# Turning a recurrent state on TensorE: eight transposes per unit in place of sixteen products with the identity, with a new written-out order

## The chip, the cores and the metric

The kernel runs on one core of one Trainium2 chip. The time is the device time of one execution in microseconds, as the median over runs. TensorE (PE in the profile) multiplies; its weight loads have a row of their own (PEld). VectorE is DVE, ScalarE is ACT, GpSimd is POOL, and SyncE (SP) issues the transfers. TensorE writes to PSUM only; ACT and DVE read PSUM and copy to SBUF.

## The reference

Two blocks follow one another. The first is a linear recurrence with a 40x40 state for each of 4 batches and 8 heads, over 768 steps:

```python
for t in range(S):
    kt, vt, rt = (k[:, :, t], v[:, :, t], r[:, :, t])
    wt, at, bt = (w[:, :, t], a[:, :, t], b[:, :, t])
    y[:, :, t] = np.einsum('bhd,bhde->bhe', rt, state)
    Sa = np.einsum('bhde,bhe->bhd', state, at)
    state_decay = state * wt[:, :, None, :] - np.einsum('bhd,bhe->bhde', Sa, bt)
    state = state_decay + np.einsum('bhd,bhe->bhde', vt, kt)
```

The second is an MLP on the 3072 tokens of 320 channels that come out: `h = x @ w_in` (320 to 2048), `g = h * sigmoid(1.702 h)`, `g @ w_out` (2048 to 320). All is fp32.

## The kernel before

The recurrence is done in 24 units: 12 blocks of 64 time steps by 2 pairs of batches. A unit `i` holds 16 heads (2 batches of 8), so the state of a unit is 16 matrices of 40x40. Each unit goes through the same steps. `decay` forms the running products of w (tiles FT, GT, G, wch, wz). `prep` scales a, k, b and forms the scores A and RV. `inverse` inverts a triangular 64x64 matrix per head in five levels (ps_N, ps_level, then ps_Q and ps_T for the off-diagonal part). `solve` brings in the state of the unit two before (the same batches, the block before): it turns the state (ps_zT), reads it with r (ps_rz), forms the known side (ps_B), solves (ps_X), and makes from it both the output and the next state (ps_y). The output x goes to DRAM and comes back with channels on the partitions (x_dram, xT_all). After every second unit the MLP of the block, `mlp`, can run: 40 pieces of ps_up, a gelu on ACT per ten of them, and 16 pieces of ps_down. The weights arrive in 8 pieces at the start and are put into fp32 by ACT, DVE and POOL (lines 489 to 507).

All products on TensorE are cut to 64 rows by at most 64 columns, so that four run at once, one in each quarter of the array. A product in fp32 shows as two loads and two matmul records. Every product but the transposes of the new version goes through the helper `mm`, line 343 (301 after), so the profile tells them apart by their tiles.

The steps around the change are in `solve`, lines 890 to 917. The raw state of the unit two before (zraw, in slots of 40 columns) is scaled by wz and written into zr, whose rows of 104 hold 64 columns for the read-out and 40 for the state. `state_turned` multiplies 16 blocks of zr, 64 rows by 40 columns, with a 64x40 identity into ps_zT, 40 rows on each half of the partitions. Two copies (line 904) bring it to zT, and `read_state` multiplies zT with r. zr itself is also an operand of ps_B.

Nothing is scheduled at run time. Each step is a task of the class `Plan` (`plan.add`), with the engines that may do it, what it reads and writes, and the PSUM pair that it holds; there are four such pairs, and a task that needs one waits in its engine's queue until it is free. The program issues the tasks in one list, and each engine runs its part of the list in that order; semaphores hold an instruction until what it needs is there. In the version before, `Plan.order` (line 103) makes the list: it steps through a model of the engines, and at each step takes the able task of lowest rank. `paced` (line 223) spreads the MLP's tasks, and `moved` (line 242) shifts ranks, releases and engines of groups of tasks by a table, `FOUND` (line 260). DMAs are issued by SP alone, in the list's order: `load_w`, `load`, the weights, x out and back, and the stores of the result.

Of the kernel before, what the change touches and what calls it, by code (L numbers as in the profile page):

```python
# [22 lines left out]
ACT = mybir.ActivationFunctionType  # L23
# [26 lines left out]
class Task:  # L50
    def __init__(self, rank, engines, fn, pair, most, size):
        self.instr, self.sbuf, self.table = engines.pop("instr", -Plan.EVENTS) + Plan.EVENTS, engines.pop("sbuf", False), engines.pop("table", None)
        self.rank, self.fn, self.pair, self.most, self.size = rank, fn, pair, most, size
        self.engines = self.may = engines
        self.after, self.then, self.release = set(), [], 0.0
        self.load = False


class Plan:

    BLOCK, FETCH, AHEAD = 256, 3460.0, 300.0
    FIRST, EVENTS = 63, 0.24
    BESIDE, LARGE, BESIDE_LARGE = 0.35, 327700, 0.5
    COLD, WINDOW, SHARE = 2.0, 2600.0, 0.45
    SWITCH = 1290.0
    DELAY = {"PE": 300.0, "DVE": 60.0, "ACT": 60.0, "POOL": 150.0, "SP": 800.0}  # L70

    BEGIN = {"PE": 0.0, "ACT": 3300.0, "DVE": 6500.0, "POOL": 10000.0, "SP": 800.0}
    LATENCY, RATE, SPREAD = 2010.0, 417.0, 1.3
# [29 lines left out]
    def order(self):  # L103
        for n, t in enumerate(self.tasks):
            t.n, t.left, t.ready, t.then = n, len(t.after), 0.0, []
        for t in self.tasks:
            for o in t.after:
                o.then.append(t)
        free = dict(self.BEGIN)
        pairs = [0.0] * self.pairs  # L110
        held, users = {}, {k: len(v) for k, v in self.of_pair.items()}
        coming = [(t.release, t.n) for t in self.tasks if not t.left]
        heapq.heapify(coming)
        able, now, wire, out, many = [], 0.0, 0.0, [], set()
        running, last, worked = [], {}, []
        table = "exp"

        def fits(t, margin=0.0):
            if t.pair is None or t.pair in held:
                return True  # L120
            clear = sum(p <= now - margin for p in pairs)
            if t.most is None:

                return clear > len({o.pair[0] for o in able if o.most is not None and o.pair not in held and not any(k[0] == o.pair[0] for k in many)})
            return clear > 0 and sum(k[0] == t.pair[0] for k in many) < t.most

        issued, begun, shared = self.FIRST, 0.0, 0.0

        def fetch(at):
            took = self.FETCH  # L130
            for _ in range(3):
                took = self.FETCH + sum(w * max(0.0, min(y, at + took) - max(x, at)) for x, y, w in running[-10:])
            return took

        def unread(t, e):

            return max((x + 60.0 for o, x in last.get(t.pair, {}).items() if o != e), default=0.0) if t.pair is not None and e != "PE" else 0.0

        def takes(t, start):

            busy = sum(max(0.0, y - max(x, start - self.WINDOW)) for x, y in worked[-60:])
            return t.engines["PE"] * (self.COLD if busy < self.SHARE * self.WINDOW else 1.0)

        def fetched(t, start):

            ns = takes(t, start) / t.instr
            at, left, block = start, t.instr, begun
            room = self.BLOCK - issued % self.BLOCK
            while left >= room:
                at += room * ns  # L150
                left -= room
                at = block = max(at, block + fetch(block))
                room = self.BLOCK
            return at + left * ns, block

        def ahead(t):

            return (issued % self.BLOCK + t.instr) * fetch(begun) / self.BLOCK - (now + takes(t, now) - begun)

        while coming or able:  # L160
            while coming and coming[0][0] <= now:
                able.append(self.tasks[heapq.heappop(coming)[1]])
            able.sort(key=lambda t: (t.rank, t.n))
            took = None
            for e in free:
                if free[e] <= now:
                    took = None
                    took = next((t for t in able if e in t.may and fits(t) and unread(t, e) <= now), None)
                    if took and e == "PE" and ahead(took) > self.AHEAD:

                        took = next((t for t in able if e in t.may and fits(t) and ahead(t) < min(self.AHEAD, ahead(took))), took)
                    if took:
                        break
            if not took:
                later = [x for x in (*free.values(), *pairs, *(unread(t, e) for t in able for e in t.may)) if now < x < float("inf")]
                later += [coming[0][0]] if coming else []
                if not later:
                    return out
                now = min(later)
                continue  # L180
            t = took
            able.remove(t)
            t.engine = e
            end = now + t.engines[e]
            if e == "ACT" and t.table:
                t.load, table = t.table != table, t.table
                end += self.SWITCH if t.load else 0.0
            if e == "PE":
                end, begun = fetched(t, now)
                worked.append((now, min(end, now + takes(t, now))))  # L190
                issued += t.instr
            if e == "POOL" or e == "DVE" and t.sbuf:

                shared = max(now, shared) + t.engines[e]
                end = max(end, shared)
            free[e] = end
            if e == "SP":
                wire = max(wire, end + self.LATENCY)
                running.append((wire, wire + self.SPREAD * t.size / self.RATE, self.BESIDE_LARGE if t.size > self.LARGE else self.BESIDE))
                end = wire = running[-1][1]  # L200
            if t.pair is not None:
                if e != "PE":
                    last.setdefault(t.pair, {})[e] = end
                if t.pair not in held:
                    held[t.pair] = next(i for i, p in enumerate(pairs) if p <= now)
                    pairs[held[t.pair]] = float("inf")
                    if t.most is not None:
                        many.add(t.pair)
                t.bank = held[t.pair]
                users[t.pair] -= 1  # L210
                if not users[t.pair]:
                    many.discard(t.pair)
                    pairs[t.bank] = end + self.DELAY[e]
            for o in t.then:
                o.ready = max(o.ready, end + (0.0 if o.engines.keys() == {e} else self.DELAY[e]))
                o.left -= 1
                if not o.left:
                    heapq.heappush(coming, (max(o.ready, o.release), o.n))
            t.start = now
            out.append(t)  # L220
        return out

    def paced(self, groups, rounds, window, share):


        best = None
        for n in range(rounds):
            out = self.order()
            end = max(t.start + t.engines[t.engine] for t in out)
            if best is None or end < best[0]:  # L230
                best = end, [(t, {**vars(t)}) for t in out]
            for g, then in zip(groups, groups[1:]):
                whole, done, begin = sum(t.engines["PE"] for t in g), 0.0, g[0].ready
                for t in g:
                    new = begin + share * (then[0].ready - begin) * done / whole - window
                    t.release = new if n == 0 else 0.5 * (t.release + new)
                    done += t.engines["PE"]
        for t, kept in best[1]:
            vars(t).update(kept)
        return [t for t, _ in best[1]]  # L240

    def moved(self, moves):

        groups = {}
        for t in self.tasks:
            key = (t.fn.__code__.co_firstlineno, t.rank, tuple(sorted(t.engines)), t.pair)
            groups.setdefault(key, []).append(t)
# [12 lines left out]
FOUND = """  # L260
# [31 lines left out]
def rwkv7_gelu_quick(ctx: ExitStack, tc: tile.TileContext, time_d, v_d, w_d, wc_d, ak_d, b_d, rv_d, w_in, w_out, out):  # L292
# [144 lines left out]
    for t in zT_t:  # L437
        nc.gpsimd.memset(t[:, DM:], 0.0)
# [742 lines left out]
```

## Time and profile before

| | |
|---|---|
| median of 3 runs | 687.27 us (685.94, 687.27, 688.87) |
| span of the profiled execution | 685.1 us (its own time isn't given beside it) |
| mean granted TensorE clock | 0.989 |
| PE busy | 649.1 us, 95% |
| DVE, ACT, POOL busy | 459.0, 323.5, 184.5 us |
| ps_up, ps_down in the chain that ended last | 29%, 30% |
| ps_zT in it | 1% |
| first and last ps_up | 73.3 and 665.8 us |

How to read it: the span goes from the first to the last instruction. A row of a group gives the engine, the operation, the tiles out<-in, the shapes and the count, then the busy time and the mean of one; behind the bar stands the engine's idle time just before and what ended it. A matmul's shape begins with the tile of the array (64*64 is 64 rows by 64 columns). A wait row says which instruction waited for which, with the total, the number of times and the longest.

### The profile page before, as it was taken

What the parts mean: (1) busy time and instruction counts of PE and PEld (TensorE: products, weight loads), DVE (VectorE), ACT (ScalarE), POOL (GpSimd) and SP (SyncE); (2) the same over time, 40 slices, a digit from 0 to 9 for tenths busy, and PEclk for the clock granted to TensorE, in tenths of its full rate; (3) what the DMA queues carried; (4) which work ended last, traced back from release to release, by engine and by line L of the source; (5) the groups of instructions that cost most, each with busy time, mean ns of one, the idle gap of its engine ahead of it and who ended that gap; (6) DMA issues with size and microseconds to landing.
All of it is one profiled execution on the core that took longest, in us unless ns stands there. A gap on an engine that the chain in (4) does not pass through costs nothing.

```text
span 685.1 us, 42187 instructions
## 1 busy us (share of the span) xinstructions
PE 649.1 (95%) x19488; PEld 563.2 (82%) x19488; DVE 459.0 (67%) x916; ACT 323.5 (47%) x670; POOL 184.5 (27%) x215
## 2 busy tenths in 40 slices
PE   3657999999999999999999999999999999999997
PEld 3556888997899899988888897788788799899895
DVE  6686989767867767857785677867666766675001
ACT  4566633454555664564455445355354454262110
POOL 5354546324123212323213130322411421300000
PEclk9989999999999999999999999999999999999999
DMA  7993434414414413432404413413411411200100
GB/s 238 314 318 118 163 119 129 122 33 127 124 42 116 144 34 107 133 90 85 132 21 125 137 40 111 145 37 115 138 40 55 136 52 43 70 14 17 56 12 20
DMA packets 35312, 69.73 MB, mean 102 GB/s; under 512 B 5440, under 2 KB 14656, under 8 KB 35136
## 3 DMA queue, kind: packets, MB, share of 16 engines
q1 hardware_dynamic: 35136, 67.03, 32.6%
q8 instruction: 153, 2.51, 1.5%
q14 instruction: 23, 0.19, 0.1%
HBM read 59.15 MB, written 7.86 MB: 98 GB/s over the span
## 4 chain that ended last, share of the span: by engine, by line
PE 90%; DVE 3%; DMA 2%; issue 2%; ACT 1%; POOL 0%; SPq 0%; ACTq 0%; DVEq 0%
PE ps_down L343 30%; PE ps_up L343 29%; PE ps_level L343 9%; PE ps_y L343 5%; PE ps_B L343 5%; PE ps_X L343 3%; PE ps_A L343 2%; PE ps_N L343 2%; PE ps_RV L343 2%; PE ps_rz L343 1%; PE ps_zT L343 1%; PE ps_cum L343 1%; PE ps_T L343 1%; DMA rv<-in_rv 1%; DMA extra<-in_w_out 1%
## 5 line engine op out<-in xcount | busy, mean ns | idle before, releaser
L343 PE MATMUL ps_up<-xT_all,w_sb 64*64 64x256 f32 x3840 | 252.4, 377 | 1.0 <-issue 0.8
L343 PE MATMUL ps_down<-w_sb,g 64*64 64x320 f32 x3072 | 240.5, 430 | 0.5 <-issue 0.3
L343 PEld LDWEIGHTS ps_up<-xT_all,w_sb 64*64 64x64 f32 x3840 | 171.7, 133 | 15.9 <-issue 1.9
L343 PEld LDWEIGHTS ps_down<-w_sb,g 64*64 64x64 f32 x3072 | 136.1, 133 | 36.3 <-issue 1.1
L755 POOL TENSOR_TENSOR EX<-ES,quads 128x512 f32<-128x512 f32 x31 | 41.7, 1345 | 117.7 <-DVE ES L748 76.5
L1034 ACT ACTIVATE g<-ps_up 128x1024 f32<-128x1024 f32 x48 | 49.2, 1026 | 49.0 <-PE ps_up L343 48.6
L797 ACT COPY W<-ps_level 128x512 f32<-128x512 f32 x56 | 32.8, 586 | 69.3 <-PE ps_level L343 67.6
L343 PEld LDWEIGHTS ps_level<-W,EX 64*64 64x64 f32 x2560 | 59.4, 134 | 5.7 <-ACT EX L753 0.2
L799 DVE TENSOR_TENSOR E<-two,ps_level 128x256 f32<-128x256 f32 x80 | 33.1, 415 | 35.7 <-ACT W L797 32.0
L343 PE MATMUL ps_level<-W,EX 64*64 64x64 f32 (+1 forms) x2560 | 56.4, 217 | 0.0
L753 ACT ACTIVATE EX<-ES,quads 128x256 f32<-128x256 f32 x80 | 36.3, 501 | 32.5 <-DVE ES L748 31.9
L665 POOL TENSOR_TENSOR ak<-ak,FT 128x512 f32<-128x512 f32 x16 | 20.6, 1288 | 76.4 <-DMA ak<-in_ak 62.3
L343 PE MATMUL ps_level<-PT,EX 64*64 64x64 f32 (+2 forms) x1280 | 33.1, 236 | 8.3 <-DVE EX L769 4.5
L343 PEld LDWEIGHTS ps_level<-PT,EX 64*64 64x64 f32 x1280 | 30.9, 139 | 11.8 <-issue 6.5
L937 ACT COPY B<-ps_B 128x416 f32<-128x416 f32 (+1 forms) x35 | 17.2, 491 | 47.2 <-PE ps_B L343 47.0
L748 DVE STREAM_TRANSPOSE ES<-E 128x256 f32<-128x256 f32 x80 | 35.2, 442 | 4.4
L343 PE MATMUL ps_y<-M,bh 64*64 64x104 f32 (+1 forms) x768 | 35.1, 247 | 0.1
L343 PE MATMUL ps_y<-RV,kh 64*64 64x104 f32 (+1 forms) x768 | 35.1, 247 | 0.0
L999 POOL TENSOR_TENSOR x<-zr,FT 128x128 f32<-128x128 f32 x48 | 25.0, 552 | 29.7 <-DVE zr L989 14.2
L673 POOL TENSOR_TENSOR kh<-time,G 128x320 f32<-128x320 f32 x19 | 16.8, 887 | 52.4 <-PE ps_y L343 39.2
L343 PE MATMUL ps_B<-RV,A 64*64 64x104 f32 (+1 forms) x768 | 29.3, 252 | 1.4 <-issue 1.4
L343 PEld LDWEIGHTS ps_B<-RV,A 64*64 64x64 f32 x768 | 25.9, 137 | 5.4 <-issue 1.6
(136 smaller groups left out, 1111.0 us busy)
## 6 DMA issues: line engine op xcount, KB each, us to landing
time<-in_time SPq DMA_DIRECT2D x24, 320.0 KB
ak<-in_ak SPq DMA_DIRECT2D x48, 160.0 KB
rv<-in_rv SPq DMA_DIRECT2D x48, 160.0 KB
xT_all<-x_dram SPq DMA_DIRECT2D x48, 160.0 KB
wc<-in_wc SPq DMA_DIRECT2D x20, 264.0 KB
logw<-in_w SPq DMA_DIRECT2D x24, 160.0 KB
RV<-in_v SPq DMA_DIRECT2D x24, 160.0 KB
b<-in_b SPq DMA_DIRECT2D x48, 80.0 KB
```

Source lines behind the costliest of these rows:

```text
L343: nc.tensor.matmul(o, lhsT, rhs, start=start, stop=True, skip_group_check=True)
L665: plan.add(R, {"DVE": 690.0, "POOL": 1270.0, "sbuf": True}, lambda t: of(t.engine).tensor_mul(ahT(), ahT(), FT_of(i)), reads=T("ak", "FT") ...
L673: plan.add(R + 4, {"POOL": 870.0, "DVE": 490.0, "sbuf": True}, lambda t, n=n, dst=dst: of(t.engine).tensor_mul(dst(i)[:, :, :D], by_head(t ...
L748: plan.add(rank, dve(256), lambda t: nc.vector.transpose(ES(n), source(t)), writes=[key("ES", n, 6)], **reads)
L753: nc.scalar.activation(dst[:, :, h], ES(n), ACT.Copy, scale=quads[:, h, :1])
L755: of(t.engine).tensor_mul(dst, ES(n).unsqueeze(2).to_broadcast([128, 8, 2, 32]), quads.unsqueeze(1).to_broadcast([128, 8, 2, 32]))
L797: plan.add(rank, any2(512), lambda t: copy(t.engine)(tiles_of(W(n + 1)), blocks(psum(t, ""), 64)), writes=[key("W", n + 1, 5)], pair=pair)
L799: plan.add(rank, dve(256), lambda t: nc.vector.tensor_sub(tiles_of(E(n + 1)), every(two32, [128, 2, 4, 32]), blocks(psum(t, ""), 64)[:, :, ...
L937: plan.add(R, any2(4 * wide), lambda t: copy(t.engine)(dst(), some(psum(t, "")[:, :, :208])), writes=[("Bv", i)] if x and c > 0 else T("B" ...
L999: of(t.engine).tensor_mul(x[:, b ^ u, b], both(i)[:, at, :64], FT_of(i)[:, at])
L1034: plan.add(-45, {"ACT": 1030.0, "table": "gelu"}, lambda t: nc.scalar.activation(g_of(c * NQ + q).rearrange("p m r n -> p r m n"), psum(t, ...
```

## The change

`state_turned` now transposes. A second product on DVE or POOL writes the scaled state once more, into a new tile zs in slots of 64 columns, 40 of them filled and 24 zero (set once at the start). Two neighbouring slots make 128 columns, and one transpose turns 64 rows by 128 columns into 128 rows by 64 columns of PSUM: eight per unit, one for each half of the rows and each of four pairs of slots. The 40 used rows on each half of the partitions are the same as before; along the columns 40 of every 64 are used, and the two copies pick these. zs has one buffer. The product into zr stays, for ps_B.

The list of tasks is no longer made by the class: a string `ORDER` holds it, one entry per task with its number, its engine and its PSUM pair, and `listed` reads it. All tasks may stand elsewhere in it, and on another engine where a task allows more than one. `order`, `paced`, `moved`, `FOUND` and their constants are gone.

```diff
+    zs_t = single("zs0", [128, 8, 64])
+    nc.gpsimd.memset(zs_t[:, :, D:], 0.0)
...
+            plan.add(R, {"DVE": 490.0, "POOL": 870.0, "sbuf": True}, lambda t: of(t.engine).tensor_mul(
+                zs_t[:, :, :D], zraw_of(i - 2), wz_of(i).unsqueeze(2).to_broadcast([128, 8, D])),
+                     reads=[("zraw", i - 2), ("wz", i)], room=[("zs", i)], writes=T("zs"))
 
             def state_turned(t):
 
                 ps = psum(t, "ps_zT")
                 for u, b in product(BITS, BITS):
-                    for e, f in QUARTERS:
-                        o, k = (2 * u + b) * D, slot(b, u, f) * 104 + 64
-                        mm(ps[CHANNELS[f], e, o:o + D], zr_of(i)[HALF[e], k:k + D], ident[HALF[e], :D], o == 0)
-            plan.add(R, pe((4, 40, D)), state_turned, reads=T("zr") + ([("clear", p)] if c == 1 else []), room=T("zT"), pair=("zT", i))
+                    for e in BITS:
+                        o, j = (2 * u + b) * 64, slot(b, u, 0)
+                        nc.tensor.transpose(ps[:, e, o:o + 64], zs_t[HALF[e], j:j + 2].rearrange("p f n -> p (f n)"), ident[HALF[e]])
+            plan.add(R, {"PE": 260.0, "instr": 16.0, "mode": 1}, state_turned, reads=T("zs"), room=T("zT"), pair=("zT", i))
             for h in CHANNELS:
                 plan.add(R, any2(320), lambda t, h=h: copy(t.engine)(
-                    zT_of(i)[h, :DM].rearrange("p (r n) -> p r n", r=2), psum(t, "")[h, :, :160]), writes=T("zT"), pair=("zT", i))
+                    zT_of(i)[h, :DM].rearrange("p (r j n) -> p r j n", r=2, n=D), psum(t, "")[h, :, :256].rearrange("p r (j n) -> p r j n", n=64)[:, :, :, :D]), writes=T("zT"), pair=("zT", i))
...
-    plan.paced(list(paces.values()), ROUNDS, WINDOW, SHARE)
-    tasks = plan.moved(MOVES)
+    tasks = plan.listed(ORDER)
     for t in tasks:
         t.fn(t)
```

The function that takes the place of the planner:

```diff
+    def listed(self, text):
+
+        assert len(text.split()) == len(self.tasks)
+        table, out, done = "exp", [], set()
+        for one in text.split():
+            e = next(e for e in ENGINES if ENGINES[e] in one)
+            n, bank = one.split(ENGINES[e])
+            t = self.tasks[int(n)]
+            assert e in t.engines and t.after <= done and (t.pair is None) == (not bank)
+            t.engine, t.bank = e, int(bank or 0)
...
+            done.add(t)
             out.append(t)
         return out
```

## The prediction

> **What bounds the kernel now.** I read the page's busy shares first, then its slices, then the chain, and then cut the span into stages.
>
> ```profile
> span 685.1 us, 42187 instructions
> PE 649.1 (95%) x19488; PEld 563.2 (82%) x19488; DVE 459.0 (67%) x916; ACT 323.5 (47%) x670; POOL 184.5 (27%) x215
> PE   3657999999999999999999999999999999999997
> PEclk9989999999999999999999999999999999999999
> ...
> q8 instruction: 153, 2.51, 1.5%
> ...
> PE 90%; DVE 3%; DMA 2%; issue 2%; ACT 1%; POOL 0%; SPq 0%; ACTq 0%; DVEq 0%
> ```
>
> TensorE is busy in every slice but the first few, and 90% of the chain is its own work. The stages (columns: stretch, length, then busy us and instruction count of PE, PEld, DVE, ACT, POOL, then granted clock, DMA share, GB/s):
>
> ```profile
> 0.00:73.20 73.20, 45.23 (x1664) 40.82 (x1664) 53.17 (x84) 41.22 (x99) 35.98 (x64) 0.91 0.76 242
> 73.20:120.00 46.80, 45.00 (x1265) 39.17 (x1265) 42.64 (x64) 21.63 (x48) 24.12 (x17) 1.00 0.41 134
> 120.00:640.00 520.00, 518.71 (x15918) 449.44 (x15914) 360.72 (x765) 256.10 (x519) 124.40 (x135) 1.00 0.30 86
> 640.00:685.00 45.00, 40.19 (x662) 33.79 (x654) 2.45 (x5) 4.52 (x5) 0.00 (x0) 0.98 0.09 21
> ```
>
> Busy time counts latency, so I price TensorE by slots: four records, one for each 64*64 tile, run side by side and the next four start a slot later. From the timeline a slot of 320 columns takes 0.269 us (32 records in 2.15), of 256 columns 0.216 (80 records in 4.32), of 104 columns 0.089, of 64 columns 0.058 (16 ps_T records in 0.23). All records at these slots make 631 us of work: about 31 before 73.2 us (the first ps_up), 40 up to 120, 516 in the 520 us to 640, and the rest after. So the middle loses some 4 us, the 73.2 to 120 stretch 6 to 7, and the front 42. Whatever a new order can win lies almost all in the front. These are its waits:
>
> ```profile
> PE ps_level L343 <- issue: 5.9, 2, 3.5
> PE ps_N L343 <- DMA ak<-in_ak: 5.8, 1, 5.8
> PE ps_level L343 <- DVE EX L769: 4.5, 5, 1.3
> PE ps_cum L343 <- ACT logw L572: 3.8, 1, 3.8
> PE ps_zT L343 <- ACT wch L615: 1.7, 1, 1.7
> ```
>
> The issue rows are holes in which no releaser shows. The instruction queue (q8: 153 packets, 2.51 MB, 16.4 KB each, that is 256 instructions of 64 bytes) fits the 39,000 TensorE instructions, so I read those holes as instruction fetch: before 73.2 us 13 such packets' worth of instructions went by, 5.6 us each.
>
> **The transposes on TensorE.** The old turning is 22 units of 32 records of 40 columns:
>
> ```profile
> 223.35 0.50 PE L343 MATMUL ps_zT<-ident,zr 64*40 64x40 f32 x30
> 223.65 0.48 PE L343 MATMUL ps_down<-w_sb,g 64*64 64x320 f32 x2
> ```
>
> The next group starts 0.30 us after it, 0.33 at 59.69 and 0.37 at 305.30; I take 0.31, so 22 x 0.31 = 6.8 us go. The chain gives ps_zT 1.0% of 685, the same. Eight transposes come in: 64 rows by 128 columns loaded, 64 columns moved. No row shows one. Low end: the two row halves side by side and one pass, so four slots of 64 columns, 0.23 us. High end: all eight one after another, each with an unhidden weight load (0.117, the 64*40 row's mean), and an array that must be empty before and after: 0.94 + 0.38 (a 256-column record to its end) + 0.20 = 1.52 us. Between them I take four slots and one exposed latency (a 64-column record lasts 0.217, its slot is 0.058, so 0.16): 0.39 us, nearest to the low end, since the records before show halves that do run side by side. 22 x 0.39 = 8.6. Net +1.8 us, ends -1.7 and +26.
>
> Groups of different columns now run into each other: in the two lines above ps_down starts while ps_zT's last two records are still to come. This is where a rule weighs in. The Trainium skill, page "TensorEngine Tiling (Array Packing)", section "Key Properties", says that a change of tiling mode, not just of tile, drains TensorE; all records before are in 64-column tiles and the transposes are 64 by 128, so by that rule each of the 22 units pays twice. No run here shows such a change. The same page, under "Restrictions", says that column tiling excludes the transpose mode for fp32, which would be why all 128 columns are taken.
>
> **Instructions.** 64 TensorE instructions per unit (32 records and 32 loads) become 16, so 22 x 48 = 1056 fewer, four of the 153 packets. Past 120 us TensorE is full, so this is hidden behind its own work and I cost it at nothing. In the front it counts only through the units 2 and 3 and lies in the next term.
>
> **The added product.** Each unit forms the scaled state a second time, into the padded tile zs: 12 units on POOL, 10 on DVE by the listing. The nearest rows are DVE 0.62 us (zr from zraw, L891) and POOL 0.89 (kh, L673): 6.2 us more on DVE at 67%, 10.7 on POOL at 27%. It stands beside the zr product that stays. The turning now waits for zs, at worst 0.89 - 0.62 = 0.27 us later, or one zr product of 0.62 later where DVE does both. What hides it is the TensorE work listed between a unit's ps_y and the ps_zT two units on: at least 2.3 us in the new order, 8 in the middle. zs has one buffer, so its next product waits for the transposes before, a unit (some 25 us) earlier. The zT copies read 40 of every 64 columns and keep 320 elements: nothing. If that cover were gone, each unit would pay up to 0.62, 14 us in all; I see no place where it is.
>
> **The order.** Counted along the listing, with slots for times. (a) Before the first ps_up there are 3232 TensorE instructions in place of 3341: 109 less, 0.43 packets at 5.6 us, -2.4 us. Bounds: 0 if no fetch ends last there, -4 with the following stretch, which is thinner too (960 instructions up to the first ps_down, in place of 1146). (b) The first ps_zT stood behind the fourth ps_cumc and waited 1.7 us, with level work and the second ps_y queued behind it; it now stands before that ps_cumc: -1.7, bounds 0 and -1.7. (c) The first ps_down comes after 46 us of TensorE work in place of 51, so the big products fill holes sooner: of the 6.6 lost in 73.2 to 120 I take 1 (bounds 0 and 4). (d) In the middle the work between a level and the next grew (medians 5.5, 4.7, 3.7, 4.2 us to 6.1, 5.7, 4.7, 4.8), and the last ps_y of a block stands 20 us ahead of its first ps_up, was 15. Little idles there, so of 4 us I take 1.5 (bounds 0 and 4). Against it: before the second ps_y, which gates the first ps_up, stand 1.7 us more TensorE work, 3.5 of DVE and 3 of POOL. On the queues of SP the loads of the first two units stand much as before, with one wc load of 264 KB put ahead of the first ak: 1 us at the 259 GB/s of the first 20 us, which the memsets that ak waits for partly cover. The tail is the same: 47.5 us of ps_up and ps_down after the last ps_y.
>
> **Sum.** +1.8 - 2.4 - 1.7 - 1.0 - 1.5 = -4.8 us. The span is 685.1 and the time differs from it by what lies around; the profiled execution's own time isn't given, and the median of the runs is 687.27, 2.2 above the span. I take the difference against the median: 682.5.
>
> **Rivals.** What a measurement can tell from no change is about 0.5%, 3.4 us.
> 1. Slower: the array empties at each change of shape and the halves don't pair. Eight slots 0.46, an exposed latency in (0.16), one out (0.16), a load after it (0.13): 0.91 us a unit, +13.2 in place of +1.8, so 694. For it: no row has two shapes of tile; against it: 0.38-us records are only part exposed. It decides from 0.61 us a unit on (the order's 6.6 eaten up), by 0.5% from 0.77.
> 2. The order wins nothing, because the front is set by loads and by chains that stand as before: 687.3 + 1.8 = 689, say 686 to 691. For it: the 5.8 us on ak and 3.8 on logw, and the like amount of work (31 us) before the first ps_up.
> 3. The order wins more: if the issue holes of the front (5.9 + 1.4 + 0.9 + 0.5 = 8.7 us) go too in place of (a): -11.1 in all, 676.
> 4. The front is longer, by the 3.5 us of DVE work put before the second ps_y, with (a) to (c) gone: 687.3 + 1.8 + 3.5 - 1.5 = 691.
>
> By the rule of that page alone, with its drains and with my paired slots, a unit would cost 0.23 + 0.16 + 0.16 + 0.13 = 0.68 and the sum would be 689: between rivals 1 and 2.
>
> **How the numbers follow.** Forecast 0.44, rival 1 0.18, rival 2 0.16, rival 3 0.14, rival 4 0.08. The forecast's own range is 678 to 686. Faster: 0.38 of the forecast and 0.14 of rival 3, 0.52. Same (683.8 to 690.7): 0.06 of the forecast and 0.12 of rival 2, 0.18. Slower: 0.18 + 0.08 + 0.04, 0.30. With both signs likely, the range for 8 in 10 goes from rival 3's far side, 673, to rival 1, 694; the extreme of eight unhidden loads is left out.
>
> **What would show it.** ps_zT with 176 records in place of 704, and the next group starting about 0.39 us after its first; 0.23 means no emptying, over 0.6 with a hole on both sides rival 1. q8 at 149 packets. The first ps_up at about 69 us (73.3 before), without the 1.7-us wait of ps_zT; at 73 or later, rival 2 or 4. From 120 to 640 PE idle of at most a microsecond or two. I am wrong if the middle stretch gets longer for the same work, or if new holes open before the first ps_up, at the DVE products in front of the second ps_y.

## The result, and the profile after

The median went from 685.34 us (18 runs, 679.29 to 688.87) to 691.99 us (18 runs, 688.47 to 699.69). The ratio is 1.0109, with a 95% interval of 1.0080 to 1.0138: the changed kernel is slower by 1.1%, some 7.5 us by the ratio and 6.65 between the two medians. The forecast was 682.5, a gain; the time lies inside the range, on the other side of no change.

The profiled execution took 695.07 us, 1.7 more than its span and 3 more than the median of its kernel. First its page, with the same parts as shown of before:

```profile
span 693.4 us, 41138 instructions
PE 658.3 (95%) x18960; PEld 523.7 (76%) x18960; DVE 445.5 (64%) x835; ACT 328.8 (47%) x718; POOL 209.4 (30%) x264
...
PE   4668999999999999999999999999999999999997
...
PEclk9969799999999999999999999999999999999999
...
q8 instruction: 149, 2.44, 1.5%
...
PE 90%; DMA 4%; issue 2%; DVE 1%; POOL 1%; ACT 1%; SPq 0%; POOLq 0%
```

TensorE has 528 matmuls and as many loads less, and is still busy for 95% of a longer span. The instruction queue moves 149 packets, four less, as forecast. In the clock's row two slices are low (6 and 7) where before had one 8. The stages, in the same columns as for before:

```profile
0.00:73.20 73.20, 46.52 (x1516) 40.60 (x1520) 55.48 (x76) 39.10 (x96) 41.39 (x69) 0.84 0.78 247
73.20:120.00 46.80, 46.80 (x1312) 38.15 (x1316) 36.70 (x57) 27.37 (x62) 25.91 (x18) 0.96 0.43 125
120.00:640.00 520.00, 516.43 (x15308) 409.23 (x15304) 348.28 (x691) 257.80 (x556) 142.07 (x178) 1.00 0.29 86
640.00:695.00 55.00, 48.56 (x836) 35.74 (x832) 5.01 (x12) 4.52 (x5) 0.00 (x0) 0.97 0.09 23
```

By 120 us the kernel has issued 2828 matmuls, and before 2929. A part of that difference is the transposes themselves, which take fewer records, so I count work in slots as the prediction did (four records of 256 columns 0.216 us, of 320 columns 0.269, of 104 0.089, of 64 0.058), with the turning of the state left at nothing in the new form. Then "lost" is time less work done:

| | first ps_up | lost by then | by 120 us | by 320 | by 470 | by 630 |
|---|---|---|---|---|---|---|
| before (span 685.1) | 73.3 | 41.8 | 44.9 | 47.3 | 48.4 | 49.3 |
| after (span 693.4) | 77.1 | 46.4 | 47.4 | 52.1 | 61.5 | 64.5 |

All counted work is 630.7 us before and 623.9 after; the 6.75 us between them are the old products. So in these two executions after loses 2.5 us more by 120 us and 12.7 more from there to 630, gains 6.75, and ends 8.4 later, which the spans bear out (8.3). The gain hoped for at the front is not there: the first ps_up comes 3.8 us later, not 4 us sooner. The waits of TensorE up to its first ps_up show what became of it, and the turning's rows what it is now (tile, then count, shortest, median and longest time in ns):

```profile
PE ps_level L301 <- DVE EX L733: 5.3, 5, 2.2
PE ps_A L301 <- DVE ak L629: 5.2, 1, 5.2
PE ps_level L301 <- issue: 4.9, 3, 3.4
PE ps_cumc L301 <- ACT logw L536: 3.7, 1, 3.7
PE ps_RV L301 <- issue: 1.9, 1, 1.9
...
PE ps_zT L868 <- POOL zs L858: 0.6, 1, 0.6
```

```profile
L868 PEld LDWEIGHTS ps_zT<-ident,zs x176: 134/139/226, 55.2 to 600.5; 64*128 64x128 f32 x176
L868 PE MATMUL ps_zT<-ident,zs x176: 221/223/366, 55.2 to 600.6; 64*128 64x64 f32 x176
```

The long waits of the front are the old ones under new names: the first ak (5.2, was 5.8), the first logw (3.7, was 3.8), and the level chain (5.3, was 4.5). The holes without a releaser come to 6.8 us (4.9 and 1.9), where before has 8.7, and the wait of the first ps_zT shrank from 1.7 to 0.6. In all TensorE stands still for 26.7 us before its first ps_up, and 28.0 in before. So in these two executions the later first ps_up isn't in the waits: the rest of what is lost by then is time in which TensorE is busy but slower than the slots, 19.7 us in after and 13.8 in before. The part on the granted clock comes back to this.

The turning itself is best read in the timeline (start, length, group):

```profile
205.45 1.28 PE L301 MATMUL ps_down<-w_sb,g 64*64 64x320 f32 x16
206.66 0.46 PE L868 MATMUL ps_zT<-ident,zs 64*128 64x64 f32 x8
207.06 0.66 PE L301 MATMUL ps_up<-xT_all,w_sb 64*64 64x256 f32 x8
```

From the first transpose to the next group are 0.40 us, almost the 0.39 that I took. But there is a second hole, ahead of it: the 16 ps_down records are four slots of 0.269, over at 206.53, and the transposes begin 0.13 later. Together a turning takes 0.53 us here, where the 32 records of products lost some 0.33.

### The profile page after: what moved, and what is told of

It is laid out like the page before. It is cut to its first block, busy times and chain, and to the rows that moved or that the text cites. A ratio compares the mean times of both kernels' runs of the same rounds, so it can differ in the third digit from the quotient of the medians.

```text
span 693.4 us, 41138 instructions
## 1 busy us (share of the span) xinstructions
PE 658.3 (95%) x18960; PEld 523.7 (76%) x18960; DVE 445.5 (64%) x835; ACT 328.8 (47%) x718; POOL 209.4 (30%) x264
## 4 chain that ended last, share of the span: by engine, by line
PE 90%; DMA 4%; issue 2%; DVE 1%; POOL 1%; ACT 1%; SPq 0%; POOLq 0%
PE ps_down L301 30%; PE ps_up L301 30%; PE ps_level L301 9%; PE ps_y L301 5%; PE ps_B L301 4%; PE ps_X L301 2%; DMA ak<-in_ak 2%; PE ps_N L301 2%; PE ps_A L301 2%; PE ps_RV L301 1%; PE ps_rz L301 1%; PE ps_zT L868 1%; DMA time<-in_time 1%; DMA extra<-in_w_in 1%; PE ps_Q L301 1%
## 5 line engine op out<-in xcount | busy, mean ns | idle before, releaser
L301 PE MATMUL ps_up<-xT_all,w_sb 64*64 64x256 f32 x3840 | 245.2, 378 | 1.2 <-issue 1.1
L301 PE MATMUL ps_down<-w_sb,g 64*64 64x320 f32 x3072 | 233.7, 430 | 0.2 <-issue 0.2
L301 PEld LDWEIGHTS ps_up<-xT_all,w_sb 64*64 64x64 f32 x3840 | 147.9, 134 | 34.2 <-issue 2.1
L301 PEld LDWEIGHTS ps_down<-w_sb,g 64*64 64x64 f32 x3072 | 122.4, 133 | 52.5 <-issue 1.0
L717 ACT ACTIVATE EX<-ES,quads 128x256 f32<-128x256 f32 x98 | 44.4, 501 | 41.3 <-DVE ES L712 37.7
L966 POOL TENSOR_TENSOR x<-zr,FT 128x128 f32<-128x128 f32 x76 | 37.3, 520 | 40.6 <-DVE zr L956 23.5
L719 POOL TENSOR_TENSOR EX<-ES,quads 128x512 f32<-128x512 f32 x19 | 24.7, 1302 | 75.2 <-DVE ES L712 64.1
L807 ACT COPY Tc<-ps_level 32x64 f32<-32x64 f32 x148 | 29.9, 202 | 23.8 <-PE ps_level L301 17.9
L629 POOL TENSOR_TENSOR ak<-ak,FT 128x512 f32<-128x512 f32 x19 | 26.7, 1406 | 47.2 <-ACT FT L588 16.4
L637 POOL TENSOR_TENSOR bh<-time,G 128x320 f32<-128x320 f32 x19 | 17.9, 944 | 60.6 <-ACT g L1001 21.2
L920 DVE TENSOR_TENSOR M<-ps_X,later 128x832 f32<-128x832 f32 (+1 forms) x24 | 23.8, 992 | 15.3 <-PE ps_X L301 15.1
```

The lines of the kernel that those rows point to most:

```text
L301: nc.tensor.matmul(o, lhsT, rhs, start=start, stop=True, skip_group_check=True)
L629: plan.add(R, {"DVE": 690.0, "POOL": 1270.0, "sbuf": True}, lambda t: of(t.engine).tensor_mul(ahT(), ahT(), FT_of(i)), reads=T("ak", "FT") ...
L637: plan.add(R + 4, {"POOL": 870.0, "DVE": 490.0, "sbuf": True}, lambda t, n=n, dst=dst: of(t.engine).tensor_mul(dst(i)[:, :, :D], by_head(t ...
L717: nc.scalar.activation(dst[:, :, h], ES(n), ACT.Copy, scale=quads[:, h, :1])
L719: of(t.engine).tensor_mul(dst, ES(n).unsqueeze(2).to_broadcast([128, 8, 2, 32]), quads.unsqueeze(1).to_broadcast([128, 8, 2, 32]))
L807: copy(t.engine)(dst, src[:, u, :, f])
```

## The experiments

I had three theories for the loss. The first: the array empties at both changes of shape, and a turning costs 0.55 us whatever the order. The second: the product into zs is not hidden. The third: the new order is worse by itself, be it through its front, through the seams of its middle, or because instruction packets begin at other places in it (theory F). In the expectations the first is theory A and the third theory B. The column "turning" below is the median time that TensorE loses to one unit's ps_zT from 120 us on, counted in slots over the turning and 1.5 us on each side.

### One part of the change at a time

**The new order with products.** The order and zs stay, and the turning is made by sixteen 64x40 products again, now reading zs.

```diff
-                    for e in BITS:
-                        o, j = (2 * u + b) * 64, slot(b, u, 0)
-                        nc.tensor.transpose(ps[:, e, o:o + 64], zs_t[HALF[e], j:j + 2].rearrange("p f n -> p (f n)"), ident[HALF[e]])
+                    for e, f in QUARTERS:
+                        o, j = (2 * u + b) * 64, slot(b, u, f)
+                        mm(ps[CHANNELS[f], e, o:o + D], zs_t[HALF[e], j, :D], ident[HALF[e], :D], o == 0)
```

> The new order, with the extra product zs, but the state turned by 16 products of 64x40 with the identity (read from zs), as before; nothing is left out. Theory A (the transposes cost about 0.53 us a unit in place of 0.31, as the slot count of the middle stretch of the trace suggests): some 5 us less than the changed kernel, so 0.3 to 0.6% slower than before. Theory B (the transposes are about neutral and the new order is what costs): as slow as the changed kernel, 1.0 to 1.2% slower than before, or slower still, since 1056 TensorE instructions come back.

Measured: 1.0147 of before (1.0095 to 1.0199), 697.96 us. By the median slower than after, though the two intervals overlap, and though a turning lost 0.46 us where the transposes lose 0.55; theory A had asked for 0.3 to 0.6%. The holes away from the turnings (stretches of 2 us between 120 and 630 that lose over 0.3) grew to 10.4 us, from 5.1 in after and 3.2 in before (about 1 us hangs on where the stretches begin). This order was written for 1056 instructions fewer, and with them back it has more stalls; that the instructions make them is not shown.

**The transposes in the order of before.** `ORDER` is the list that the planner of before makes, with zs put on DVE just ahead of zr (617d ahead of 616d in one unit; a letter is an engine, d DVE, g POOL, and a number behind it a PSUM pair). The lines are against the changed kernel. In the traces of the runs with this list, DVE, ACT and POOL run the sequence of before with zs added and nothing else.

```diff
-2s 10s 11s 148s 3s 7s 8s 104a 160a 20s 9s 5a 4s 90p0 12s 89p1 13s 0d 14s 91a0 1d 15s 16s 17s 6a 97d 18s 92a1 19s 95d 29s 93s
...
+2s 3s 10s 11s 7s 4s 8s 104a 160a 15s 9s 5a 6a 12s 89p0 90p1 13s 14s 0d 91a1 93s 1d 16s 148s 17s 92a0 95d 18s 94a 19s 96d
...
+406s 561a 256p0 571g 559s 546d3 257p0 569d 572g 542p1 558d 617d 616d 258p0 407s 543a1 794s 498d2 710s 578p1 499d2 702p3
...
```

> The order of before, written out as a list, with the eight transposes in place of the sixteen products, and the extra product zs on DVE just before the product into zr. Theory A: 22 x 0.22 = 4.8 us slower than before, 0.7%. Theory B: within 0.3% of before. If zs on DVE costs on the path, this and the next run are both slower than before by it.

Measured: 1.0104 (1.0056 to 1.0152), 694.6 us. A turning lost 0.57 us, as in the new order (0.55): its price belongs to the operation and not to the order. And with the same work the two orders take the same time, 1.0104 and 1.0109. The two intervals together leave the new order a gain of at most some 3.5 us, and the 6.6 that I gave it lies outside.

**Only zs added.** The order of before, zs on DVE, and the sixteen products reading zs (the same edit of `state_turned` as above).

> The order of before with the extra product zs on DVE, and the 16 products with the identity reading zs: the cost of zs alone. Theories A and B: within 0.3% of before, since DVE is busy 67%. A third theory, that 22 more DVE products of 0.62 us lie on the path: up to 2% slower.

Measured: 1.0051 (1.0020 to 1.0082), 691.18 us; a turning 0.33, as in before. The second product on DVE is not free there: 22 of them,

```profile
L865 DVE TENSOR_TENSOR zs<-zraw,wz x22: 446/488/1562, 56.6 to 594.5; 128x320 f32<-128x320 f32 x22
```

at 0.49 us, and half a per cent of the time, which is 3.5 us. In its profile TensorE stands still for 1.9 us from 120 to 630 us, and for 1.2 in before, so where the 3.5 us are lost does not show in one row.

**Only the order.** The new order with the old work: zs is not formed, zr is made on DVE where zs stood in the list (12 of the 22 zs stood on POOL), and the sixteen products read zr. The lines are against the changed kernel, without those of the list.

```diff
-            plan.add(R, {"DVE": 490.0, "POOL": 870.0, "sbuf": True}, lambda t: of(t.engine).tensor_mul(
-                zs_t[:, :, :D], zraw_of(i - 2), wz_of(i).unsqueeze(2).to_broadcast([128, 8, D])),
+            plan.add(R, {"DVE": 490.0, "POOL": 870.0, "sbuf": True}, lambda t: None,
...
+                    for e, f in QUARTERS:
+                        o, k = (2 * u + b) * 64, slot(b, u, f) * 104 + 64
+                        mm(ps[CHANNELS[f], e, o:o + D], zr_of(i)[HALF[e], k:k + D], ident[HALF[e], :D], o == 0)
```

> The new order with the old work: zs is gone, the product into zr stands (on DVE) where zs stood, and 16 products with the identity read zr, exactly what before computes. The sum of the prediction said that the order alone is worth -6.6 us, so 1% faster than before. Against it: the new order with zs and the products was 1.5% slower and its trace had 10 us of holes in the middle where TensorE waited for no releaser; if these come from the order meeting 1056 more instructions than it was made for, this is 0.8 to 1.5% slower than before.

Measured: 1.0118 (1.0077 to 1.0160), 692.14 us. This is the plainest sign of where the prediction went wrong: with the work of before, the new order is slower by 8 us, where I had it faster by 6.6. Two things limit it. "Order" includes the engines: 339 of the 2724 tasks stand on another engine than in the list of before, 208 of them moved between DVE and ACT. And the list was written for the transposes, so it may suit the old work badly; with the new work it is neither faster nor slower than the old list with zs on DVE.

### Where zs is made

**zs on POOL**, against the transposes in the order of before:

```diff
-406s 561a 256p0 571g 559s 546d3 257p0 569d 572g 542p1 558d 617d 616d 258p0 407s 543a1 794s 498d2 710s 578p1 499d2 702p3
+406s 561a 256p0 571g 559s 546d3 257p0 569d 572g 542p1 558d 617g 616d 258p0 407s 543a1 794s 498d2 710s 578p1 499d2 702p3
...
```

> The order of before with the transposes, and zs on POOL in place of DVE. If the cost of zs is DVE time, this is 0.3 to 0.5% faster than the same with zs on DVE, so 0.5 to 0.7% slower than before; if its cost is that the turning waits for it, POOL's 0.89 us in place of 0.62 makes it the same or slower, 1.0 to 1.3%.

Measured: 1.0057 (1.0028 to 1.0087), 688.69 us, against 1.0104 with zs on DVE. One zs takes longer on POOL (median 0.92 us), and still the run is 0.47% less slow than with zs on DVE. The two intervals overlap, so that POOL is the better place is likely and not shown. At this place the operations cost 0.57%, 3.9 us.

**zs only from the fifth unit on**, products, order of before: the units before it read zr. The lines are against the run with only zs added.

```diff
-            plan.add(R, {"DVE": 490.0, "POOL": 870.0, "sbuf": True}, lambda t: of(t.engine).tensor_mul(
+            plan.add(R, {"DVE": 490.0, "POOL": 870.0, "sbuf": True}, lambda t: None if i < 4 else of(t.engine).tensor_mul(
...
+                        if i < 4:
+                            o, k = (2 * u + b) * 64, slot(b, u, f) * 104 + 64
+                            mm(ps[CHANNELS[f], e, o:o + D], zr_of(i)[HALF[e], k:k + D], ident[HALF[e], :D], o == 0)
```

> The order of before with zs and the 16 products reading it, but units 2 and 3 (the first two that have a state, in the front) without zs, reading zr. If the 0.5% that zs cost in the order of before came from the two DVE products in the front, this is within 0.2% of before; if it comes from the middle, still 0.4 to 0.5% slower.

Measured: 1.0051 (1.0021 to 1.0080), the same as with zs everywhere. So most of the half per cent seems to be paid by DVE in the middle, where TensorE looked like the only limit. It is not settled: the intervals would let the front have most of it, and in the one profiled execution with zs everywhere 2.7 of the 4.8 us over the profile of before are lost by 120 us.

### What one turning is made of

**A second set of eight transposes**, into the free half of the same PSUM bank pair, right behind the first:

```diff
+                for u, b in product(BITS, BITS):
+                    for e in BITS:
+                        o, j = 256 + (2 * u + b) * 64, slot(b, u, 0)
+                        nc.tensor.transpose(ps[:, e, o:o + 64], zs_t[HALF[e], j:j + 2].rearrange("p f n -> p (f n)"), ident[HALF[e]])
```

> The changed kernel with a second set of eight transposes right behind the first, into the free half of the same PSUM banks; nothing is left out, the second set is read by nobody. If a unit's 0.55 us is the pace of the transposes themselves, the group costs 1.1 us; if four slots of 0.058 are their pace and the rest is emptying the array, 0.78 to 0.82, and the trace shows the sixteen records about 0.034 us apart.

```profile
203.06 1.24 PE L301 MATMUL ps_down<-w_sb,g 64*64 64x320 f32 x13
204.23 0.46 PE L868 MATMUL ps_zT<-ident,zs 64*128 64x64 f32 x8
204.53 0.41 PE L872 MATMUL ps_zT<-ident,zs 64*128 64x64 f32 x8
204.87 0.66 PE L301 MATMUL ps_up<-xT_all,w_sb 64*64 64x256 f32 x8
```

Measured: a turning 0.80 us in place of 0.55 (690.39 us in one execution, against 685.13 for before). Eight more transposes cost 0.25 us, what four slots of 64 columns cost (0.23). The two halves of the rows do run side by side.

**Four 64x64 products in the middle of the transposes, and the same four behind them.** Both do the same work, into columns that nothing reads; the first changes shape twice more. The diff is that of the first; in the second the call stands behind the loop.

```diff
+                def products():
+                    for e, h in QUARTERS:
+                        mm(ps[HALF[h], e, 256:320], zs_t[HALF[e], h], ident[HALF[e]], False)
+                for u, b in product(BITS, BITS):
+                    if (u, b) == (1, 0):
+                        products()
+                    transposes(u, b)
```

> The changed kernel with four ordinary 64x64 products (8 records, two slots, 0.12 us of work, into free columns that nobody reads) put in the middle of the eight transposes, so that the shape changes four times a unit and not twice. If each pair of changes costs about 0.28 us, the group takes 0.28 us more than in the next run, 6 us over 22 units; if changes are free, the same as the next.

> The control of the run before: the same four products behind the eight transposes, so the shape changes twice a unit. The group costs 0.55 us as in the changed kernel, and 0.12 for the products.

The timeline of the first:

```profile
210.17 0.34 PE L868 MATMUL ps_zT<-ident,zs 64*128 64x64 f32 x4
210.43 0.34 PE L301 MATMUL ps_zT<-ident,zs 64*64 64x64 f32 x8
210.71 0.34 PE L868 MATMUL ps_zT<-ident,zs 64*128 64x64 f32 x4
210.97 0.66 PE L301 MATMUL ps_up<-xT_all,w_sb 64*64 64x256 f32 x8
```

and of the second:

```profile
207.26 0.46 PE L868 MATMUL ps_zT<-ident,zs 64*128 64x64 f32 x8
207.65 0.34 PE L301 MATMUL ps_zT<-ident,zs 64*64 64x64 f32 x8
207.81 0.61 PE L301 MATMUL ps_up<-xT_all,w_sb 64*64 64x256 f32 x8
```

Measured: 0.97 us a turning split, 0.67 joined, so 0.30 for a pair of changes of shape, 0.15 each (699.96 and 692.66 us in one execution each). 0.25 for the transposes and 0.30 for going there and back are 0.55: the whole turning is accounted for. In the lines, each set of four transposes and the eight products between them take 0.26 to 0.28 us from start to next start, where two slots are 0.12. The eight products behind the joined set, in the shape of what follows, have ps_up behind them after 0.16.

**Ordinary products in the new shape**: `mm` in place of the transpose.

```diff
-                        nc.tensor.transpose(ps[:, e, o:o + 64], zs_t[HALF[e], j:j + 2].rearrange("p f n -> p (f n)"), ident[HALF[e]])
+                        mm(ps[:, e, o:o + 64], zs_t[HALF[e], j:j + 2].rearrange("p f n -> p (f n)"), ident[HALF[e]], o == 0)
```

> The changed kernel with the eight transposes replaced by eight ordinary products with the identity of the same shape, 64 rows by 128 columns, which take two passes each: the change of tile shape stays, the transpose goes. If the emptying of the array at a change of shape is what costs, a unit costs 0.53 us plus a second pass of four slots, 0.23: 5 us more than the changed kernel, 1.8% slower than before. If wide tiles cost nothing in changing and transposes themselves are slow, a unit costs 0.46 us or less and this is faster than the changed kernel.

```profile
L301 PEld LDWEIGHTS ps_zT<-ident,zs x352: 182/188/189, 56.8 to 612.7; 64*128 64x128 f32 x176
L301 PE MATMUL ps_zT<-ident,zs x352: 272/272/321, 56.8 to 612.7; 64*128 64x64 f32 x176
```

Measured: 1.0275 (1.0233 to 1.0316), 707.28 us; a turning 1.20, where I had expected 0.76 with the emptying and 0.46 without. In this shape an fp32 product shows as two records, with loads of 0.188 us, and the transpose as one; why the second pass costs 0.65 and not 0.23 was not taken apart. So the transposes are by far the better way to use the wide shape. What they cannot beat is thirty-two records that never leave the shape of everything around them.

### What is wrong with the new order

**The old front, and the new middle**; and the other way round. The list of the one up to the first ps_down, then the rest of the other, with the transposes in both. The diff shows the seam of the first, against the order of before; the second takes the lines above that place from the new order and keeps the rest.

```diff
-231p1 397p2 232a1 76d 244p0 563s 398a2 77d 492p1 245p0 399d2 79g 493d1 246p0 481d 384p1 233p2 385a1 234p2 235p2 84a
+231p1 397p2 232a1 76d 488d 497p0 500a0 498d0 499d0 501g 398d2 563s 244p3 502d 245p3 331p0 481d 503a 77d 490g 485s 332d0
...
```

> The transposes and zs, the list of before (with zs on DVE before zr) up to the first ps_down, and the rest of the tasks in the new order. Theory: the two fronts are worth the same, and the new order wins nothing anywhere: 0.8 to 1.3% slower than before, like the changed kernel. Rival: the new front is what loses, since the first ps_up comes at 77 us in place of 73: then this is 0.5% faster than the changed kernel, some 0.5% slower than before.

> The transposes and zs, the new list up to the first ps_down, then the rest in the order of before. If the two fronts are worth the same, 0.8 to 1.3% slower than before, like the changed kernel, like its mirror image (1.2%) and like the order of before with the transposes (1.0%). If the new front wins the 4 to 5 us that the prediction gave it, 0.3 to 0.5% slower.

Measured: 1.0117 (1.0054 to 1.0180), 693.34 us, and 1.0220 (1.0183 to 1.0256), 699.48 us. The second is worse than either of its expectations. Neither part carries a gain into the other list. The seam has a price of its own (the first ps_down of the second came at 100.4 us, in before at 94.4 and in after at 92.3), so these two do not say how much of the loss is in which part.

**Half a packet and a whole packet of instructions more at the start**, in each of the two orders: dummy products of 32 columns ahead of all else, whose output nothing reads. 32 of them are 128 TensorE instructions, half of the 256 that one packet of the instruction queue holds; 64, with 16 rounds in place of the 8 of the diff, are 256.

```diff
+    blank = single("blank", [128, 64])
+    nc.vector.memset(blank, 0.0)
...
+    spare = banks.tile([128, 2, 512], FP32, tag="pair3", name="spare")
+    for _ in range(8):
+        for e, h in QUARTERS:
+            mm(spare[HALF[h], e, :32], blank[HALF[e]], blank[HALF[e], :32], True)
```

> The changed kernel with 32 small products of a zeroed tile (128 TensorE instructions, half of one of the instruction queue's packets of 256) ahead of everything, in the first 4 us where TensorE waits for its first operand; their result is read by nobody. Theory F: the new order is fitted to where the packets of instructions begin, and what it loses or wins hangs on that; then this differs from the next run, which moves them by a whole packet, by 0.4% or more. Rival: the order's cost is its own (dependences, queues), and both are 1.0 to 1.2% slower than before.

> The same with 64 small products, 256 instructions, one whole packet: the phase of the packets against the list is that of the changed kernel. Both theories: 1.0 to 1.3% slower than before, a packet more being fetched at the start, where TensorE waits anyway.

> The kernel before with the 32 small products ahead. Theory F holds for it as well, since its order was made with the packets in the model: 0.4% or more slower than before. Rival: within 0.2%.

> The kernel before with 64 small products ahead, a whole packet. Both theories: within 0.3% of before.

Measured, against before: the new order 1.0086 (1.0056 to 1.0117) and 1.0106 (1.0070 to 1.0141); the order of before 1.0045 (1.0021 to 1.0069) and 1.0002 (0.9972 to 1.0032). Half a packet costs the order of before 3.1 us, and a whole packet, twice the work, nothing: so work at the start that shifts the list by half a packet costs something that twice as much does not, as theory F has it for that order. In the profiles the half packet's loss lies in the middle (7.9 us from 120 to 630, against 4.9 with the whole packet, counted as in the table of lost time); no row shows where a packet begins. The new order shows no clear difference between the two, nor from after's 1.0109, so theory F doesn't hold for it as far as half a packet can tell; other shifts were not tried.

**The granted clock** was not tried by itself. These are two stretches of the front, of after and then of before (the number behind the five engines is the clock):

```profile
34.00:48.00 14.00, 8.59 (x232) 7.29 (x236) 12.35 (x16) 7.21 (x16) 9.22 (x5) 0.58 0.97 295
62.00:76.00 14.00, 10.45 (x331) 9.25 (x325) 11.56 (x17) 7.76 (x17) 6.56 (x10) 0.68 0.77 238
```

```profile
34.00:48.00 14.00, 10.21 (x362) 9.57 (x359) 12.67 (x25) 9.50 (x22) 5.71 (x5) 0.76 1.01 318
62.00:76.00 14.00, 12.14 (x464) 10.96 (x457) 13.78 (x22) 8.24 (x15) 5.76 (x6) 1.00 0.58 182
```

In these executions the clock falls to half in three stretches of the front, 27 us in after and 14 in before. That it costs time shows in the 18 kept traces: up to the first ps_up, each microsecond in which TensorE is busy at half clock goes with 0.46 us more of busy time over the slots (correlation 0.89). But the 27 and 14 are chance of two executions as much as of the two orders. The ten traces with the new front have 10.5 to 27 us of it before their first ps_up (mean 20), the eight with that of before 14 to 27 (mean 19). The run of the old work in the new order, 1.2% slower than before, has the 10.5.

Over all executions the mean granted clock was 0.9828 with the new front (60 executions of ten kernels, standard error 0.0005) and 0.9876 with that of before (70 of seven kernels, 0.0005; before itself the same, 73). Kernel by kernel the means overlap, 0.981 to 0.987 and 0.985 to 0.989. Within one kernel, executions at a lower mean clock are longer: in before by 3.3 us for each 0.01 (73 executions, correlation -0.51), in the others together by 2.9. So 0.0048 of clock goes with about 1.5 us. That is a correlation, and what makes the clock fall is not shown.

## Why the prediction was wrong

The step that failed is the order, put at -6.6 us. The runs show no gain from it: with the new work both orders take the same time (1.0109 and 1.0104, a gain of at most some 3.5 us), the first ps_up comes 3.8 us later where I had it 4 sooner, and with the old work the new order is 8 us slower. Two terms were too small besides, the transposes (+1.8, measured +4.8) and zs on DVE (nothing, measured 3.5 for 22 of them).

**The transposes (+1.8 predicted, +4.8 measured).** Four slots for the eight and one exposed latency made 0.39. The slots were right (0.25 against 0.23), the one latency was right (0.40 from the first transpose to the next group), and the mis-sized term is the one that I left out, the emptying ahead of the transposes. It costs another 0.15, so a turning takes 0.55, and 22 x (0.55 - 0.33) = 4.8 us. The sentence of the Trainium skill, page "TensorEngine Tiling (Array Packing)", section "Key Properties", that I had set beside this, that a change of tiling mode drains TensorE, is borne out in both directions: 0.30 us for going there and back. I had made 0.68 of it with a load behind, and the runs show 0.55. Nothing in the trace of before spoke against it, since no row had two shapes; I let the row with the same shape on both sides decide.

**Rival 1 (halves don't pair, array empties, 694)** was half right: it empties, but the halves do pair, and 0.55 is below the 0.61 from which it was to decide. That the time of 692 is near its 694 is luck.

**zs (nothing predicted).** On POOL that may have held; on DVE it did not: 0.5% for 22 of them in the order of before. That zs stands "beside" was argued from the busy share of DVE, 67%, and from TensorE work that covers one zs; which chain pays for them the runs do not show. In after 12 of the 22 are on POOL and 10 on DVE; what those ten cost in its order was not measured apart.

**The instructions (nothing predicted).** In the order of before, operations and zs on POOL cost 3.9 us (1.9 to 6.0), which does not differ clearly from the 4.8 of the turnings by count, so a gain from fewer instructions is not shown. In the new order they may matter more: with the products back (and zs kept) it loses 0.4% more, though these intervals overlap.

**The order (-6.6 predicted).** This is the step that failed, with the sign. Point by point:

- (a) Four packets went, and by the traces 96 instructions fewer stand before the first ps_up. The holes without a releaser there are 6.8 us against 8.7 in this pair of executions, but over the kept traces 7.8 in the ten with the transposes and 8.1 in the seven with the products of before: next to nothing of the 2.4. The price of 5.6 us a packet was the front's length divided by its packets, and no row shows that a fetch takes this long. Nor is the term the order's own: the 96 instructions go with the transposes in either order.
- (b) The wait of the first ps_zT did shrink, by 1.1 us, and that did not bring the first ps_up forward. In the kept traces TensorE has lost 43.3 to 47.2 us by its first ps_up with the new front (ten traces, mean 45.7) and 40.4 to 43.6 with that of before (eight, mean 42.2). Of the 3.5 between the means 2.1 are standing still, and the rest is slower pace.
- (c) The first ps_down came at 92.3, 2.1 us sooner, and from the first ps_up to 120 us after loses 1.0 where before loses 3.1. This is the only part of the order that gave what it was said to, though the 6.6 us that I read as lost there were 3.1 by the count above. By 120 us most of the later start is made up: 44 to 49 us lost with the new front, 44 to 48 with that of before, without the two runs that have a seam.
- (d) I priced a middle that lost 4 us as if it could only lose less. It lost 17 in after, of which 19 turnings at a mean of 0.60 explain 11.4 (work and all). That is the work and not the order: with the same work the order of before loses 17 there too. With the old work the new order does lose more in the middle, by 3.2 us.

Rival 2 had the reason nearest, a front set by loads and by chains that stand as before. Rival 4 had the sign, a first ps_up later by about the 3.5 us of DVE work; that this work is what made it later is not shown.

**What adds up and what stays open.** After is 7.5 us slower; by count 4.8 are the turnings. The other 2.7 are zs, the instructions and the order together. Set against runs with the same operations in the order of before, which cost 7.1 us with zs on DVE and 3.9 with zs on POOL, the new order, with 12 of its zs on POOL, costs between nothing and 3.6. The lower mean clock of its front goes with 1.5 us, by correlation alone. With the old work the order loses 8 us, and the clock is a small part of it: its six executions have 0.9835 against 0.9875, which goes with 1.3 us. The profiled one, 4.6 us above the profile of before, loses 2.0 us more by the first ps_up; its turnings are at 0.37 us in the median and 0.47 in the mean (0.33 and 0.35 in before), so some of them wait, which over 19 makes 2.3 us; and its holes are 0.6 longer. These are readings of single executions, and executions with the same front lose from 43.3 to 47.2 us by the first ps_up. What in the list, or in the 339 tasks on other engines, makes the rest is open.

**What would have shown it** was in the prediction: a first ps_up "at 73 or later" came, and so did a middle that "gets longer for the same work", in the run of the old work in the new order.

## What to carry to other kernels

An operation that works in another shape of the array pays for emptying it on the way in and on the way out, 0.15 us each here, so it must save more than that, or several such operations must stand together: eight more transposes behind the first eight cost only 0.25 us. A full engine does not make work on the others free: 22 products of 0.49 us on an engine busy for 67% cost half a per cent here, so run an added product by itself, on each engine that may do it, before calling it hidden. And the slack that a listing shows (instructions fewer, a wait shorter) is not a gain until the wait that comes next is known; run the old order with the new work, and the new order with the old work, to see what the order is worth.

## What the runs showed that I had not expected

- An fp32 transpose of 64 rows by 128 columns is one load (0.139 us) and one matmul record (0.223), where an ordinary fp32 product of the same shape is two of each, at 0.188 and 0.272. A unit's turning takes 0.55 us with the one and 1.20 with the other.
- 128 instructions of next to no work ahead of a 685-us kernel cost 0.45% (1.0021 to 1.0069), and 256 of them nothing (1.0002).
- Half-speed stretches of the clock before the first ps_up add up to anything from 10.5 to 27 us in 18 traces of much the same work, and a microsecond that TensorE is busy in them goes with 0.46 us lost.
